# Second MoE layer in two stages with g in DRAM, and its output by seven products for eight

## The chip, the cores and the metric

The kernel runs on one core of a Trainium2 chip. The metric is device time in microseconds of one launch; the median of several runs counts. Engines: PE (TensorE), DVE (VectorE), ACT (ScalarE), POOL (GpSimd) and SP (SyncE, which here issues nearly all DMAs, in order).

## The reference

The kernel computes attention through a small memory, then two MoE-like layers, all in fp32:

```python
xn = x / rms * rms_g
g = xn @ w_gate;  silu = g * (1.0 / (1.0 + np.exp(-g)));  val = xn @ w_val
x = (silu * val) @ w_out                 # first layer, d_ff 1536
h = x @ w_in                             # second layer, d_ff 2048
out = np.maximum(h, 0.0) ** 2 @ w_out2
```

There are 4608 tokens of 512 values. The change touches the second layer and the work that prepares it.

## The kernel before, in words

Every fp32 operand of a matmul is split into a high and a low part (`split`: the high part on ACT, the low part on DVE or, where said, on POOL), and a product is three matmuls: high x high, high x low, low x high.

**First layer** (`phase_a`): 192 items n, 24 for each of 8 batches. An item is 12 matmuls of 288 columns for g and v, one silu on ACT, a product on DVE, a split (low part on POOL) and 12 matmuls into y for the item before. At four places of an item, `slot` runs steps of a plan. In the last batch (n = 168 to 191) the loop also loads x for the second layer and makes its sums (`x2_step`, one an item), and the first W_in set.

**Second layer** (`phase_b`): tokens go in four pairs of blocks of 512 and a last pair of 256. For each pair, eight steps q each take two slices of 128 hidden values of W_in. A 2x2 block product (two token blocks by two slices, split also along the 512 values) is done by seven products for eight: A11·X11, A12·X21, S2·T2, S3·T3, S1·T1, S4·X22, A22·T4, with S sums of W_in blocks and T sums of x blocks. A product is six matmuls (two kk of 128 values), so a step is 42. DVE combines the results into four blocks of h, relu and square give g.

The output g·W_out is plain: `mm_z` (L1184 to L1186), three matmuls of 128x512 for each slice f and each 128 tokens. For the first block of a pair (`z`) g stays in SBUF, and pieces of four `mm_z` stand between the h products; for the second block (`zz`) g goes to DRAM (`gd`), comes back on ACT's queue (`gb`), is split and multiplied after the pair's steps. W_in is loaded and split again for every pair (its S sums come back split from DRAM, `sd`). The 16 slices of W_out are split at the start of this stage (`wo2_next`). The order on each engine is the order in which the code is written (manual_schedule). A DMA on SP also waits for the eighth DMA before it.

## Time and profile before

| | us |
|---|---|
| median of three runs | 1612.98 (1611.53 to 1613.99) |
| span of the profiled execution | 1610.1 |
| first matmul of the second layer | at 853.30 |
| last matmul | at 1603.54 |

The profiled execution's own time is its span; the runs' median lies 2.9 us above it. The profile counts an engine as busy while instructions of it run; matmuls overlap in their pipeline, so that the distance between two starts, not the printed duration, says what one more matmul costs. PEclk is the TensorE clock that was granted, in tenths of full speed; windows give it as a fraction.

### The profile page before, as it was taken

What the parts mean: (1) busy time and instruction counts of PE and PEld (TensorE: products, weight loads), DVE (VectorE), ACT (ScalarE), POOL (GpSimd) and SP (SyncE); (2) the same over time, 40 slices, a digit from 0 to 9 for tenths busy, and PEclk for the clock granted to TensorE, in tenths of its full rate; (3) what the DMA queues carried; (4) which work ended last, traced back from release to release, by engine and by line L of the source; (5) the groups of instructions that cost most, each with busy time, mean ns of one, the idle gap of its engine ahead of it and who ended that gap; (6) DMA issues with size and microseconds to landing.
All of it is one profiled execution on the core that took longest, in us unless ns stands there. A gap on an engine that the chain in (4) does not pass through costs nothing.

```text
span 1610.1 us, 26490 instructions
## 1 busy us (share of the span) xinstructions
PE 1556.0 (97%) x10298; PEld 1311.0 (81%) x10298; DVE 953.7 (59%) x1645; ACT 592.8 (37%) x1208; POOL 386.6 (24%) x415
## 2 busy tenths in 40 slices
PE   6788999999999999999999999999999999999998
PEld 3556798888979889898998887888788878887887
DVE  5755645657365465625457876666666655666465
ACT  2666435354453544434343334211321133122322
POOL 0475534344353444333322210000000000000000
PEclk7688999999999999999999999999999999999999
DMA  9997583654657464324124465345534453445353
GB/s 265 281 310 279 196 233 134 211 189 154 189 205 200 166 187 140 118 71 146 55 75 172 174 240 168 96 140 179 176 116 144 155 179 108 158 160 177 97 165 99
DMA packets 143021, 269.92 MB, mean 168 GB/s; under 512 B 30704, under 2 KB 72944, under 8 KB 136752
## 3 DMA queue, kind: packets, MB, share of 16 engines
q1 hardware_dynamic: 129440, 248.43, 47.4%
q10 hardware_dynamic: 13328, 19.54, 4.1%
q8 instruction: 81, 1.33, 0.3%
q14 instruction: 44, 0.36, 0.1%
q0 software_dynamic: 128, 0.26, 0.1%
HBM read 208.28 MB, written 59.90 MB: 167 GB/s over the span
## 4 chain that ended last, share of the span: by engine, by line
PE 84%; DVE 5%; DMA 3%; ACT 3%; POOL 1%; issue 1%; SPq 0%; ACTq 0%; POOLq 0%; DVEq 0%
PE y L827 6%; PE y L828 5%; PE y L829 5%; PE z L1184 5%; PE z L1186 5%; PE z L1185 4%; PE h_S L1020 4%; PE h_S L1018 4%; PE h_S L1019 4%; PE zz L1186 3%; PE v L811 3%; PE h_A L1018 3%; PE zz L1185 3%; PE zz L1184 3%; PE h_A L1020 3%; PE h_A L1019 3%
## 5 line engine op out<-in xcount | busy, mean ns | idle before, releaser
L71 POOL TENSOR_TENSOR ul<-sl,uh 128x288 fp32r<-128x288 f32 x192 | 163.1, 850 | 387.2 <-ACT uh L67 384.2
L827 PE MATMUL y<-uh,woh 128*128 128x288 f32 x768 | 236.8, 308 | 0.0
L828 PE MATMUL y<-uh,wol 128*128 128x288 f32 x768 | 228.7, 298 | 0.0
L829 PE MATMUL y<-ul,woh 128*128 128x288 f32 x768 | 227.4, 296 | 0.0
L861 DVE TENSOR_TENSOR sl<-sl,v 128x288 f32<-128x288 f32 x192 | 86.2, 449 | 209.2 <-PE v L813 153.2
L67 ACT ACTIVATE gh<-c 128x512 fp32r<-128x512 f32 (+1 forms) x96 | 53.8, 561 | 404.2 <-DVE c L1053 395.9
L827 PEld LDWEIGHTS y<-uh,woh 128*128 128x128 f32 x768 | 146.0, 190 | 17.7 <-issue 16.8
L1192 POOL DMA_DIRECT2D out_dram<-os_last x4 | 2.2, 552 | 656.5 <-DVE os_last L1203 656.5
L828 PEld LDWEIGHTS y<-uh,wol 128*128 128x128 f32 x768 | 146.5, 191 | 0.7
L829 PEld LDWEIGHTS y<-ul,woh 128*128 128x128 f32 x768 | 146.0, 190 | 0.0
L67 ACT ACTIVATE uh<-sl 128x288 fp32r<-128x288 f32 x192 | 85.2, 444 | 163.6 <-DVE sl L861 162.9
L857 ACT ACTIVATE sl<-g 128x288 f32<-128x288 f32 x192 | 78.5, 409 | 170.7 <-PE g L813 163.0
L811 PE MATMUL g<-anh,wph 128*128 128x288 f32 x384 | 119.2, 310 | 12.3 <-ACT sl L857 9.9
L1184 PE MATMUL z<-bzh,gh 128*128 128x512 f32 x320 | 126.1, 394 | 0.0
L1186 PE MATMUL z<-bzh,gl 128*128 128x512 f32 x320 | 125.7, 393 | 0.0
L1185 PE MATMUL z<-bzl,gh 128*128 128x512 f32 x320 | 125.0, 391 | 0.0
L811 PE MATMUL v<-anh,wph 128*128 128x288 f32 x384 | 120.0, 312 | 1.7 <-DVE sl L861 1.7
L812 PE MATMUL v<-anl,wph 128*128 128x288 f32 x384 | 115.0, 299 | 0.0
L812 PE MATMUL g<-anl,wph 128*128 128x288 f32 x384 | 114.9, 299 | 0.1
L813 PE MATMUL v<-anh,wpl 128*128 128x288 f32 x384 | 114.7, 299 | 0.0
L813 PE MATMUL g<-anh,wpl 128*128 128x288 f32 x384 | 113.7, 296 | 0.0
L556 DVE TENSOR_TENSOR wpl<-wp,wph 128x512 fp32r<-128x512 f32 x96 | 61.4, 682 | 87.0 <-ACT wph L550 86.9
(217 smaller groups left out, 3749.5 us busy)
## 6 DMA issues: line engine op xcount, KB each, us to landing
w<-w SPq DMA_DIRECT2D x48, 1024.0 KB, 6.7
si<-w_i SPq DMA_DIRECT2D x80, 256.0 KB, 2.8
q<-in_q_dram SPq DMA_DIRECT2D x128, 144.0 KB, 5.1
gd<-c SPq DMA_DIRECT2D x64, 256.0 KB, 2.0
gb<-gd ACTq DMA_DIRECT2D x64, 256.0 KB, 3.6
y<-ys SPq DMA_DIRECT2D x16, 576.0 KB, 3.3
raw_i<-in_moe_w_in_dram SPq DMA_DIRECT2D x16, 512.0 KB, 4.1
raw_z<-in_moe_w_out_dram SPq DMA_DIRECT2D x16, 512.0 KB, 4.4
```

The costliest lines, as they stand in the source:

```text
L67: nc.scalar.activation(hi, src, AF.Copy)
L71: eng.tensor_tensor(lo, src, hi.bitcast(F32), op=ALU.subtract)
L811: nc.tensor.matmul(out, wh[:, r, cs], ah[:, r], start=(r == 0), stop=False)
L812: nc.tensor.matmul(out, wh[:, r, cs], al[:, r], start=False, stop=False)
L813: nc.tensor.matmul(out, wl[:, r, cs], ah[:, r], start=False, stop=(r == NR - 1))
L827: nc.tensor.matmul(y, hi[:, cs], uh, start=first, stop=False)
L828: nc.tensor.matmul(y, lo[:, cs], uh, start=False, stop=False)
L829: nc.tensor.matmul(y, hi[:, cs], ul, start=False, stop=last)
L1018: nc.tensor.matmul(out, wh[:, cs], xh, start=(kk == 0), stop=False)
L1184: nc.tensor.matmul(y[c], gh[:, cs], oh, start=(f == 0), stop=False)
L1185: nc.tensor.matmul(y[c], gh[:, cs], ol, start=False, stop=False)
L1186: nc.tensor.matmul(y[c], gl[:, cs], oh, start=False, stop=(f == NF2 - 1))
```

## The change

- **Preparation in the last batch.** From item 171 on, `slot` runs one piece of a list at each of its four places. The list (`last_batch`) has the two times seven x steps, all eight sets of W_out and two of W_in. A set is two raw slices (256 KB each, two buffers shared with x, `xr`), four sums of 128x256 on POOL that go where nothing else is kept, three splits (a, c, b of 256 or 512, and 1024 columns), and a store of the split set, 128x3584 or 1.8 MB, to DRAM (`wd`), followed on SP by the load of the set after next.
- **h stage** (`phase_h`). The steps of pairs 0 and 1 run interleaved, then those of 2, 3 and 4, by the strings in `STEPS`, so a W_in set serves two or three pairs. Sets 2 to 7 are made in the first group and read back from DRAM in the second. All of g goes to DRAM. Relu and square are two ACT passes for three of four blocks. Products rotate over eight PSUM banks. For pairs 1 to 4 the differences of x are on POOL.
- **Output stage** (`phase_z`). 18 runs of 128 rows (of both blocks of a pair), each in four groups of two q. A group loads g (two DMAs of 128x4x128), makes four sums (two DVE, two POOL), splits 1792 columns (ACT, DVE) and does seven products of 128x256 for two q, three matmuls each: 42. `z_out` combines them after a run. W_out sets T0 to T7 are loaded in the last steps of the h stage (`wt_load`) into the buffers of pairs 2 and 3's x sums; the g load of every third group uses that of pair 4's.

PE, where before an output piece follows a step's second product:

```order
L1018 MATMUL h_1_A_10531<-X21h_1_10068,wiha_10452 128x512
L1019 MATMUL h_1_A_10531<-X21l_1_10069,wiha_10452 128x512
L1020 MATMUL h_1_A_10531<-X21h_1_10068,wila_10453 128x512
L1184 MATMUL z_0_10518<-bzh_10396,gh_0_10439 128x512
L1185 MATMUL z_0_10518<-bzl_10397,gh_0_10439 128x512
L1186 MATMUL z_0_10518<-bzh_10396,gl_0_10440 128x512
L1184 MATMUL z_1_10519<-bzh_10396,gh_0_10439 128x512
L1185 MATMUL z_1_10519<-bzl_10397,gh_0_10439 128x512
L1186 MATMUL z_1_10519<-bzh_10396,gl_0_10440 128x512
L1018 MATMUL h_1_S_10551<-T2h_0_9864,wihb_10468 128x512
```

PE at the end of the last h step, where the output stage now begins (Wr is W_in read back, T an output-weight set, S the split sums of g):

```order
L1081 MATMUL h_7_A_13819<-x_41_11424,Wr_13214 128x256
L1082 MATMUL h_7_A_13819<-x_41_11424,Wr_13214 128x256
L1083 MATMUL h_7_A_13819<-x_41_11424,Wr_13214 128x256
L1275 MATMUL z_0_13839<-T_13364,S_13610 128x256
L1276 MATMUL z_0_13839<-T_13364,S_13610 128x256
L1277 MATMUL z_0_13839<-T_13364,S_13610 128x256
L1275 MATMUL z_0_13839<-T_13364,S_13610 128x256
L1276 MATMUL z_0_13839<-T_13364,S_13610 128x256
L1277 MATMUL z_0_13839<-T_13364,S_13610 128x256
L1275 MATMUL z_1_13840<-T_13364,S_13610 128x256
L1276 MATMUL z_1_13840<-T_13364,S_13610 128x256
L1277 MATMUL z_1_13840<-T_13364,S_13610 128x256
```

The output matmuls have left the h steps, and are of 256 columns.

ACT in the last batch before (sl is the silu, uh and X.. or T.. high parts):

```order
L67 ACTIVATE X22h_1_10105<-xr_1_9945 128x512
L857 ACTIVATE sl_10116<-g_10109 128x288
L67 ACTIVATE uh_10126<-sl_10116 128x288
L67 ACTIVATE T3h_1_10144<-xt_1_10142 128x512
L857 ACTIVATE sl_10155<-g_10148 128x288
L67 ACTIVATE uh_10165<-sl_10155 128x288
L67 ACTIVATE T1h_1_10182<-xr_1_9945 128x512
L857 ACTIVATE sl_10193<-g_10186 128x288
L67 ACTIVATE uh_10203<-sl_10193 128x288
```

ACT there now, with the last two W_in sets (Wi, made from si):

```order
L79 ACTIVATE uh_10243<-sl_10231 128x288
L79 ACTIVATE Wi_10240<-si_10159 128x256
L79 ACTIVATE Wi_10240<-si_10159 128x1024
L898 ACTIVATE sl_10281<-g_10263 128x288
L79 ACTIVATE uh_10293<-sl_10281 128x288
L79 ACTIVATE Wi_10297<-si_10219 128x512
L79 ACTIVATE Wi_10297<-si_10219 128x256
L79 ACTIVATE Wi_10297<-si_10219 128x1024
L898 ACTIVATE sl_10322<-g_10313 128x288
L79 ACTIVATE uh_10337<-sl_10322 128x288
L898 ACTIVATE sl_10360<-g_10353 128x288
L79 ACTIVATE uh_10370<-sl_10360 128x288
```

The high parts of three pieces of a weight set stand between the silus of successive items.

SP in the last batch before:

```order
L843 DMA y_13_84<-ys_9433 128x1152
L980 DMA xr_0_9594<-y_0_71 128x2x288
L980 DMA xr_0_9594<-y_1_72 128x2x224
L980 DMA xr_0_9594<-y_1_72 128x2x64
L980 DMA xr_0_9594<-y_2_73 128x2x288
L980 DMA xr_0_9594<-y_3_74 128x2x160
L922 DMA si_0_9600<-w_i_93 128x512
L922 DMA si_1_9602<-w_i_95 128x512
L843 DMA y_14_85<-ys_9913 128x1152
L980 DMA xr_1_9945<-y_0_71 128x2x288
```

SP there now (wdz are the stored sets, sz the raw slices):

```order
L100 DMA wdz_9519<-Wz_9833 128x3584
L956 DMA sz_9871<-w_z_106 128x512
L956 DMA sz_9871<-w_z_108 128x512
L100 DMA wdz_9520<-Wz_9893 128x3584
L956 DMA sz_9924<-w_z_110 128x512
L956 DMA sz_9924<-w_z_112 128x512
L100 DMA wdz_9521<-Wz_9948 128x3584
L956 DMA sz_9984<-w_z_114 128x512
L956 DMA sz_9984<-w_z_116 128x512
L884 DMA y_14_85<-ys_10038 128x1152
L100 DMA wdz_9522<-Wz_10005 128x3584
```

Each store stands ahead of the load of the set after next.

SP at the end of the h stage now:

```order
L1171 DMA gd_6_9564<-c_4_6_13733 128x256
L1171 DMA gd_6_9564<-c_4_6_13710 128x256
L1013 DMA T_13757<-wdz_9524 128x3584
L1171 DMA gd_7_9565<-c_4_7_13766 128x256
L1013 DMA T_13771<-wdz_9525 128x3584
L1171 DMA gd_7_9565<-c_4_7_13802 128x256
L1171 DMA gd_7_9565<-c_4_7_13814 128x256
L1171 DMA gd_7_9565<-c_4_7_13791 128x256
L1216 DMA sr_13829<-gd_4_9530 128x4x128
L1216 DMA sr_13829<-gd_5_9531 128x4x128
L1216 DMA sr_13832<-gd_6_9532 128x4x128
L1216 DMA sr_13832<-gd_7_9533 128x4x128
```

The loads of the last two output-weight sets and the last g stores stand ahead of the g loads of group 2 (sr).

The diff, cut:

```diff
+NQ = NF2 // 2
+NPAIR = NB // 2 + 1
+PART = 7 * 2 * P
...
+STEPS = [
+    [(p, int(q)) for name, q in zip(names[::2], names[1::2]) for p in [order.index(name) + base]]
+    for order, base, names in (
+        ("AB", 0, "A0A1A2B0B1A3B2A4B3A5B4A6A7B5B6B7"),
+        ("ABC", 2, "A0A1A2B0C0B1C1A3B2C2A4B3C3A5B4C4A6A7B5C5B6B7C6C7"),
+    )
+]
...
-        eng.tensor_tensor(lo, src, hi.bitcast(F32), op=ALU.subtract)
+        self.after(partial(eng.tensor_tensor, lo, src, hi.bitcast(F32), op=ALU.subtract))
+
...
+        if self.later is None:
+            f()
+        else:
+            self.later.append(f)
...
+        low, self.low = self.low, []
+        self.later = self.low
+        if self.side:
+            self.side.pop(0)()
+        self.later = None
+        for f in low:
+            f()
...
+        self.wd = {(k, q): dram.tile([P, 2 * PART], F32, name=f"wd{k}{q}") for k in "iz" for q in range(NQ)}
+        self.gd = [
+            [dram.tile([P, 4, self.width(p)], F32, name=f"gd{p}_{q}") for q in range(NQ)] for p in range(NPAIR)
+        ]
+        self.w2_raw, self.w2_out, self.wi, self.wt, self.x2, self.xr = {}, {}, {}, {}, {}, {}
+        self.side = self.last_batch()
...
-            self.phase_b()
+            self.phase_h()
+            self.phase_z()
...
+        if n >= NI * (B - 1) + 3:
+            self.piece()
...
-                self.x2_load(0, 0)
...
-            elif i == 13:
-                self.x2_load(0, 1)
-            if 6 <= i < 13:
-                self.x2_step(0, 0, i - 6)
-            elif 15 <= i < 22:
-                self.x2_step(0, 1, i - 15)
-            elif i == 5:
-                self.wi2_sums(0, 0)
-            elif i in (13, 14, 22):
-                self.wi2_split(0, 0, "abc"[(13, 14, 22).index(i)])
-            elif i == 23:
-                self.wi2_load(0, 1)
-                self.wo2_next(0)
...
+        out = [partial(self.chain, partial(self.x2_load, 0, 0), load("z", 0))]
+        out += then(x2(0), partial(self.x2_load, 0, 1)) + then(self.w2_pieces("z", 0, 0), load("z", 1))
+        out += then(x2(1), load("z", 2))
+        for q in range(1, NQ):
+            after = load("z", q + 2) if q < NQ - 2 else load("i", q + 2 - NQ)
+            out += then(self.w2_pieces("z", q, q % 2), after)
+        out += then(self.w2_pieces("i", 0, 0), partial(self.x2_load, 1, 0))
+        out += then(self.w2_pieces("i", 1, 1), load("i", 2))
+        return out
...
+        t = self.wb.tile([P, 2, 2, DM], F32, tag="xr", bufs=2, name=f"s{kind}{q}")
         for i in range(2):
...
+            self.nc.sync.dma_start(t[:, 0, i], self.w2d[kind, 2 * q + i])
...
+        out = [partial(self.w2_sums, kind, q, i) for i in range(2)]
+        return out + [partial(self.w2_split, kind, q, slot, part) for part in "acb"]
...
+            eng.tensor_tensor(s[:, 3], a12, s[:, 1], op=ALU.subtract)
+        elif half == 0:
+            eng.tensor_tensor(s[:, 0], a12, a11, op=ALU.subtract)
+            eng.tensor_tensor(s[:, 1], a22, s[:, 0], op=ALU.subtract)
+        else:
+            eng.tensor_tensor(s[:, 2], a22, a12, op=ALU.subtract)
+            eng.tensor_tensor(s[:, 3], s[:, 1], a21, op=ALU.subtract)
...
+        if part == "a":
+            self.w2_out[kind, q] = self.w_tile(slot, f"W{kind}{q}")
...
-            for x, d in zip(t, self.sd[q]):
-                self.nc.sync.dma_start(d, x.bitcast(F32))
+            src, o = raw[:, 1].rearrange("p a n -> p (a n)"), 3 * n
+        elif kind == "i":
+            src, o = (s0, 0) if part == "a" else (s1[:, n:DM], 2 * n)
+        else:
+            src, o = (s0[:, 0:n], 0) if part == "a" else (s1, n)
+        e = o + src.shape[-1]
+        self.split(t[:, o:e], t[:, PART + o : PART + e], src)
+        if part == "b":
+            del self.w2_raw[kind, q]
+            if kind == "i":
+                self.wi[q] = t
+            self.after(partial(self.nc.sync.dma_start, self.wd[kind, q], t.bitcast(F32)))
...
+        t = self.w_tile((NQ + q) % 3, f"Wr{q}")
+        self.nc.sync.dma_start(t.bitcast(F32), self.wd["i", q])
...
+        pool = self.wb2 if q // 4 else self.wb
+        t = pool.tile([P, 2 * PART], F32R, tag=f"x{q // 4}_{q % 4}", name=f"T{q}")
+        self.nc.sync.dma_start(t.bitcast(F32), self.wd["z", q])
...
+        eng = nc.gpsimd if p else nc.vector
...
+        self.split(hi, lo, x, lo_engine="pool" if p and i in (2, 3) else "dve")
...
+        at(0, "A0", x2(1, 0), xl(1, 1))
+        at(0, "A1", w2(2), wl(3))
+        at(0, "A2", x2(1, 1), wl(4))
+        at(0, "B1", w2(3), wl(5))
...
+        at(1, "A1", x2(3, 0, 5), partial(self.s_load, 0))
+        at(1, "A1", x2(3, 1, 0, 3))
+        at(1, "A2", x2(3, 1, 3), partial(self.s_load, 1))
...
+            plan[g, k].insert(0, partial(self.wi_load, q))
+        for q, name in enumerate(("B5", "C5", "B6", "B7", "C6", "C6", "C7", "C7")):
+            at(1, name, [partial(self.wt_load, q)])
+        at(1, "B6", self.s_sums(0))
+        at(1, "B7", self.s_split(0))
+        at(1, "C6", self.s_sums(1))
+        at(1, "C7", self.s_split(1))
...
+        tags = ("g", "v", "att", "att", "y0", "y1", "y2", "y3")
...
+            def store(c, blk, engine="act"):
+                if engine == "act":
+                    nc.scalar.activation(c, c, AF.Relu)
+                    nc.scalar.activation(c, c, AF.Square)
...
-                c11 = work("c", 4, f"c11_{p}_{q}", w)
-                nc.vector.tensor_tensor(c11, b2, p1, op=ALU.add)
...
-                    self.wi2_split(np, nq, "a")
-                piece()
-                b5 = product("S1", "T1")
-                nc.vector.tensor_tensor(u, b5, u, op=ALU.add)
...
-                self.mm_z(y, self.gs[p, f0], f0, c)
-            if not wide:
...
-            for f in range(NF2 + 1):
-                gb_load(f + 7)
-                if f < NF2:
-                    self.gs.pop((p, f), None)
-                    key = ("b", p, f)
-                    hi = self.wb2.tile([P, T], F32R, tag="uh", bufs=3, name=f"gbh{p}_{f}")
-                    lo = self.wb2.tile([P, T], F32R, tag="ul", bufs=3, name=f"gbl{p}_{f}")
-                    self.split(hi, lo, loaded[f])
-                    self.gs[key] = (hi, lo)
-                if f:
-                    self.pieces += z_pieces(2 * p + 1, y, ("b", p, f - 1), f - 1)
...
+                    nc.vector.scalar_tensor_tensor(c, c, 0.0, c, op0=ALU.max, op1=ALU.mult)
+                nc.sync.dma_start(self.gd[p][q][:, blk], c)
+
+            b1 = product("A11", "X11")
+            p1 = work("cp", 3, f"p1_{p}_{q}")
+            nc.scalar.activation(p1, b1, AF.Copy)
...
+            c11 = work("c", 6, f"c11_{p}_{q}")
+            nc.vector.tensor_tensor(c11, b2, p1, op=ALU.add)
+            store(c11, 1)
...
+            t = self.wb.tile([P, 8, 2, P], F32, tag="xr", bufs=2, name=f"sr{g}")
+        else:
+            t = self.wb2.tile([P, 8, 2, P], F32, tag="x4_1", name=f"sr{g}")
+        for i in range(2):
+            self.nc.sync.dma_start(t[:, 0:4, i, :], self.gd[p][2 * qg + i][:, :, r * P : (r + 1) * P])
...
+            if first:
+                nc.vector.tensor_tensor(t[:, 6], t[:, 1], t[:, 0], op=ALU.subtract)
+                nc.vector.tensor_tensor(t[:, 5], t[:, 3], t[:, 6], op=ALU.subtract)
+                nc.gpsimd.tensor_tensor(t[:, 4], t[:, 0], t[:, 3], op=ALU.add)
+            else:
+                nc.gpsimd.tensor_tensor(t[:, 7], t[:, 2], t[:, 5], op=ALU.subtract)
...
+            t = self.sr.pop(g)[:, 1:8].rearrange("p i q n -> p (i q n)")
+            o = self.w_tile((g + 1) % 3, f"S{g}")
+            self.split(o[:, 0:PART], o[:, PART : 2 * PART], t)
...
+        for f in [partial(self.s_load, 2), partial(self.s_load, 3)] + self.s_sums(2):
+            f()
...
+            self.s_load(g + 4)
+            side = self.s_sums(g + 3) + self.s_split(g + 2)
+            s = self.ss.pop(g)
...
+                    nc.tensor.matmul(out, sh, th, start=first, stop=False, **kw)
+                    nc.tensor.matmul(out, sh, tl, start=False, stop=False, **kw)
+                    nc.tensor.matmul(out, sl, th, start=False, stop=last, **kw)
+
+                mm(0, 0, 0, 0)
+                mm(0, 1, 6, 2)
...
+        o0 = self.wb2.tile([P, T], F32, tag="c", bufs=6, name=f"o{run}_0")
+        nc.vector.tensor_tensor(pair(o0), pair(z1), twice(p1), op=ALU.add)
+        u = self.wb2.tile([P, T], F32, tag="cp", bufs=3, name=f"zu{run}")
+        nc.vector.tensor_tensor(pair(u), pair(z2), twice(o0[:, n:T]), op=ALU.add)
...
+        nc.vector.tensor_tensor(o0[:, n:T], z0[:, n:T], u[:, n:T], op=ALU.add)
+        self.out_rows(p, r, 0, o0, (nc.sync, nc.gpsimd) if last else (nc.sync,))
+        nc.vector.tensor_tensor(o1[:, n:T], z2[:, n:T], u[:, 0:n], op=ALU.add)
+        nc.vector.tensor_tensor(o1[:, 0:n], u[:, 0:n], z3[:, 0:n], op=ALU.subtract)
+        self.out_rows(p, r, 1, o1, (nc.scalar, nc.sync) if last else (nc.sync,))
```

## Rows read from the trace of the kernel before

**Rows 1.** The page: busy time by engine, and the granted clock in 40 slices.

```profile
PE 1556.0 (97%) x10298; PEld 1311.0 (81%) x10298; DVE 953.7 (59%) x1645; ACT 592.8 (37%) x1208; POOL 386.6 (24%) x415
...
PEclk7688999999999999999999999999999999999999
```

**Rows 2.** Windows: busy time of each engine, granted clock, DMA share, GB/s.

```profile
core 0: us, PE busy (x) PEld busy (x) DVE busy (x) ACT busy (x) POOL busy (x), PEclk, DMA share, GB/s
772.00:808.00 36.00, 36.00 (x279) 34.98 (x279) 12.12 (x21) 14.48 (x33) 13.34 (x18) 1.00 0.19 61
...
853.30:1603.80 750.50, 747.81 (x3410) 615.16 (x3408) 486.40 (x808) 199.21 (x375) 22.54 (x25) 1.00 0.46 153
```

**Rows 3.** Timeline of PE: first matmuls of two steps with no piece between.

```profile
1014.86 0.39 PE L1018 MATMUL h_A<-X11h,wiha 128*128 128x512 f32 x1
...
1030.03 0.40 PE L1018 MATMUL h_A<-X11h,wiha 128*128 128x512 f32 x1
```

**Rows 4.** Groups by form: output matmuls of first and second blocks, busy, mean ns.

```profile
L1184 PE MATMUL z<-bzh,gh 128*128 128x512 f32 x320 | 126.1, 394 | 0.0
...
L1184 PE MATMUL zz<-bzh,gbh 128*128 128x512 f32 x256 | 100.3, 392 | 2.1 <-ACT gbh L67 2.1
```

**Rows 5.** Timeline of PE: matmuls of 288 and of 256 columns in a row.

```profile
702.74 0.30 PE L811 MATMUL g<-anh,wph 128*128 128x288 f32 x1
...
703.94 0.29 PE L811 MATMUL v<-anh,wph 128*128 128x288 f32 x1
...
1527.55 0.28 PE L1018 MATMUL h_S<-T2h,wihb 128*128 128x256 f32 x1
...
1528.97 0.39 PE L1184 MATMUL z<-bzh,gh 128*128 128x512 f32 x1
```

**Rows 6.** Timeline of DVE and ACT in the last batch; 835.18 is item 187.

```profile
787.32 0.46 DVE L861 TENSOR_TENSOR sl<-sl,v 128x288 f32<-128x288 f32 x1 [2.73 <-PE v L813]
790.54 0.45 DVE L861 TENSOR_TENSOR sl<-sl,v 128x288 f32<-128x288 f32 x1 [2.76 <-PE v L813]
...
835.18 0.41 ACT L857 ACTIVATE sl<-g 128x288 f32<-128x288 f32 x1 [0.66 <-PE g L813]
```

**Rows 7.** Timeline of POOL: the four sums of a W_in set, twice.

```profile
850.56 0.74 POOL L938 TENSOR_TENSOR si_s<-si 128x256 f32<-128x256 f32 x1
...
852.76 0.74 POOL L941 TENSOR_TENSOR si_s<-si,si_s 128x256 f32<-128x256 f32 x1
...
872.27 0.74 POOL L938 TENSOR_TENSOR si_s<-si 128x256 f32<-128x256 f32 x1 [18.77 <-DMA si<-w_i]
...
875.32 0.74 POOL L941 TENSOR_TENSOR si_s<-si,si_s 128x256 f32<-128x256 f32 x1
```

**Rows 8.** Groups by form: splits of W_in and a difference of x, busy, mean ns.

```profile
L67 ACT ACTIVATE wiha<-si 128x512 fp32r<-128x512 f32 x40 | 24.7, 617 | 0.0
...
L71 DVE TENSOR_TENSOR wilc<-si,wihc 128x256 fp32r<-128x256 f32 x40 | 17.1, 428 | 0.8 <-ACT wihc L67 0.8
...
L71 DVE TENSOR_TENSOR wilb<-si_s,wihb 128x1024 fp32r<-128x1024 f32 x8 | 9.8, 1221 | 1.8 <-ACT wihb L67 1.8
L67 ACT ACTIVATE wihb<-si_s 128x1024 fp32r<-128x1024 f32 x8 | 8.5, 1057 | 9.3 <-POOL si_s L941 9.2
...
L997 DVE TENSOR_TENSOR xt<-xr 128x512 f32<-128x512 f32 x8 | 5.5, 686 | 0.0
```

**Rows 9.** DMA issues (KB each, us to landing), and windows as in rows 2.

```profile
si<-w_i SPq DMA_DIRECT2D x80, 256.0 KB, 2.8
...
xr<-y SPq DMA_DIRECT2D x14, 288.0 KB, 4.1
...
sd0h<-wihb SPq DMA_DIRECT2D x1, 512.0 KB, 3.4
...
60.00:80.00 20.00, 14.17 (x213) 10.60 (x213) 16.23 (x26) 13.36 (x25) 10.65 (x9) 0.63 0.83 258
100.00:120.00 20.00, 15.82 (x110) 12.56 (x102) 12.21 (x20) 11.60 (x24) 15.13 (x13) 0.91 1.05 323
824.00:826.00 2.00, 2.00 (x17) 2.00 (x16) 0.97 (x2) 1.36 (x3) 0.81 (x1) 1.00 1.05 409
```

More of the change, by code (lines that the diff above doesn't have):

```diff
@@ new lines, in last_batch, with x2, then, load @@
+    def last_batch(self):
+        def x2(kk):
+            return [partial(self.x2_step, 0, kk, i) for i in range(7)]
+        def then(pieces, *loads):
+            return pieces[:-1] + [partial(self.chain, pieces[-1], *loads)]
+        def load(kind, q):
+            return partial(self.w2_load, kind, q)
+        out = [partial(self.chain, partial(self.x2_load, 0, 0), load("z", 0))]
[7 more added lines that the diff above has]
+        return out
@@ L1004, in x2_step @@
         else:
             k, x = "T4", x21
[L1006 to L1012 removed]
+            eng.tensor_tensor(x, x21, x22, op=ALU.subtract)
+        j = X_ORDER.index(k)
+        hi, lo = (self.x2[p, kk, hl][:, j, 0:w] for hl in range(2))
```

451 lines of the change are left out of this document (209 added, 242 removed).

## The prediction

> **What bounds the kernel now.** I read the page's busy shares first: PE is busy 97% of the span, and its granted clock is at nine tenths or more in all slices but the first four [rows 1]. Then the windows: from the first product of the second layer, 853.30, to its last, PE works 747.81 of 750.50 us, with DVE at 486 and ACT at 199 [rows 2]. So this stage is a chain of matmuls with no holes; it gets shorter only by fewer columns, and any work of DVE, ACT, POOL or DMA that fits beside PE is free. The batch before it is the same: 36.00 of 36.00 us busy [rows 2], one item each 3.22 us [rows 6]. There too the change can only add. Its order is therefore: what do fewer columns give, and does the preparation that pays for them fit?
>
> **Part 1, columns.** Before, the second layer has 1344 h matmuls of 512 columns (4 pairs x 8 steps x 42), 336 of 256 (last pair), and (320 + 256) x 3 = 1728 output matmuls of 512 [rows 4]. The prices: an h step without pieces runs from 1014.86 to 1030.03 with 66 matmuls of 512, so 15.17 / 66 = 0.2298 us [rows 3]; twelve matmuls of 256 take 1528.97 − 1527.55 = 1.42, 0.1183 each [rows 5]. The durations that the rows print (0.39, 0.28) overlap; the distance of starts is the price. h costs 1344 x 0.2298 + 336 x 0.1183 = 348.6 and stays. The output part now is 750.5 − 348.6 = 401.9. After, it is 72 groups (18 runs of 128 rows from both blocks of a pair, four groups of q each; 7 products x 2 q x 3 matmuls = 42 in a group), 3024 matmuls of 256: 3024 x 0.1183 = 357.7. **Gain 44.2.** Bounds: nine matmuls of 288 take 1.20 [rows 5], 0.1333 each; scaled from 288 to 256 with the slope between 256 and 288 unknown, 0.1194 at worst (gain 41); a price strictly by columns, 0.2298 / 2 = 0.1149, would gain 54, but the twelve of 256 already show more, so I end the range half way, at 49.
>
> **Part 2, the last batch.** The W_in of two steps, all eight output-weight sets and their sums are now made there, one piece per slot, four slots an item. 85 slots hold 65 pieces, so by slots it fits. By engine time it does too: ten sets need POOL 10 x 2.94 (four sums, 850.56 to 852.76 + 0.74 [rows 7]). What does not fit is the chain through two raw buffers. A set's raw is 0.52 MB, its sums overwrite half of the buffer, and SP, which issues in order, has: store of set q (1.835 MB, waits for the last low part), load of set q+2, store of q+1. So each buffer goes round like this:
> - landed to last low part: sums 2.94, hi of 128x1024 1.06, lo 1.22 [rows 7, 8], hand-overs 0.3: 5.5;
> - low part to landed: store and load, 2.36 MB at 409 GB/s, the most that a window shows while transfers queue [rows 9], 5.77; a 256 KB load takes 2.8 on its own [rows 9], of which 0.64 is this rate's transfer, so 2.1 fixed; issue 0.3: 8.2.
>
> A round is 13.7 us and makes two sets; their ten pieces stand in 2.5 items, 8.0 us of PE. The preparation falls behind PE by 5.7 us a round.
>
> The start: seven x2 pieces, now four an item, need seven low parts and four differences of 0.69 [rows 8] on DVE, 7.6 us against 5.6 by slots. By hand: first x2 set done 793.1, second load landed 798 and done 806.6, last low part of set z1 809.6, so z3 landed 817.8, and with three more rounds (z5, z7, i1) i1 landed 858.9. PE feels it through ACT: the wide hi part of i1 stands on ACT ahead of the silu of item 187, and the low parts of POOL behind the sums. Sums and hi, 4.3, put that silu at 863.2; now it starts at 835.18 [rows 6]. That is 28.0, of which 2.4 is PE's lead over ACT: **+26**. Bounds: +13.5 if the lag of DVE and the hand-overs vanish and only the transfers count; +34 if sums take the 3.79 that they take from 872.27 to 875.32 + 0.74, beside DVE [rows 7], on each round, with the lag.
>
> A rule bears on this. The Trainium skill (GPSIMD Engine Reference, section 1, Specifications) says that POOL shares its SBUF interfaces with VectorE and contends with DVE instructions that read two SBUF inputs, which every low part does. Rows 7 agree in kind: 2.94 alone, 3.79 beside DVE. By the rule on every set the stage would give the +34.
>
> **Part 3, the start of the output stage.** Let E be the end of the last h step. The output-weight sets T4 to T7 go into the buffers of pair 3's X sums, free only when pair 3 ends, two steps of 42 x 0.1183 = 4.97 before E. They are 7.34 MB, 17.9 us at 409 GB/s; with 2.1 fixed and the g stores between them on SP, 1.2, T7 lands at E + 11.3. The load for group 2 uses a buffer of pair 4's X sums, free at E, and stands behind T7 on SP: landed about E + 15.7 (issue 0.3 and the 4.1 that a strided load of 288 KB takes [rows 9]). Its two DVE sums (0.43 each [rows 8]), the last POOL sum 0.74, hi of 1792 columns (1.057 + 768 x 0.44/512 = 1.72) and lo (2.02 the same way) end at E + 21. Groups 0 and 1 keep PE until E + 9.9. **+11**, bounds +4 (the load overtakes T7 on the 16 queues) and +15 (rate of rows 9's slower window).
>
> **Part 4, the rest.** The h stage loses its mix of pieces: a step is 42 x 0.2298 = 9.65 us of PE, in which ACT at the fullest has 14 passes of 0.617 (one copy, three relu and three square, seven hi), 8.6; DVE seven combinations, one relu-square and five low parts, 9.0; POOL four differences and two low parts, 5. That is under 9.65 with eight banks rotating: **0**, bounds −4 and +6. Its DMA, 1.05 MB of g and at most 1.8 MB of weights a step, is 7 us at 409 GB/s: covered by the same step; without that cover a reload would hold PE directly. In the output stage a group is 4.97 of PE against ACT 1.7 plus a share of the combination, DVE 3.5, POOL 1.5 to 2.5, DMA 1.3: covered. What ran beside PE before (z's splits, W_in prepared for each pair, gb loads, the 128 stored rows) costs and gives nothing. After a stall the clock has to rise again: rows 9 show 0.63 while PE is busy 14.17 of 20 us, so two stalls of 10 to 26 us may be followed by slow stretches, **+2** (0 to 6).
>
> **Sum.** 1610.1 − 44.2 + 26 + 11 + 2 = 1604.9 for the profiled execution. The median of the runs, 1612.98, lies 2.9 above that execution: **1608**.
>
> **The rivals.**
> A (slower): the transfers do not get 409 GB/s. That row is 2 us long; in the long full window 100 to 120 the 16 DMA engines are at 1.05 of their time at 323 GB/s [rows 9]. Against it: those early transfers are in smaller pieces. At 323 store and load take 7.3 instead of 5.77, over 3.5 rounds +5.4, and part 3 another +4.8: 1618. It decides against me from about 335 GB/s down, where the sum crosses 1616.
> The Trainium skill (DMA: Bandwidth & Descriptors, Specifications) gives about 358 GB/s as the HBM limit for one core; the row with 409 lies over that, in a window too short to be sure. By 358 the sum would be 1613.
> B (slower): TensorE falls to its 1.2 GHz level inside the last batch, as PE then works 8.0 us in 13.7, 58%; rows 9 show 0.63 at 71%. At half the clock the work of a round takes 16 us rather than 8.0, more than the 13.7, so PE, not the chain, sets the pace: four rounds of 16 − 13.7 give +9, and up to +13 with the climb behind them; at +12, 1620. Against it: PE's work comes in bursts at full density, unlike the first stage's.
> C (faster): both stalls are mostly hidden, by transfers of several queues overlapping (last batch +13.5, start of output +5, clock 0): 1610.1 − 44.2 + 18.5 + 2.9 = 1587. For it: sd0h's 512 KB land in 3.4 [rows 9], nearly without a fixed part if they overlap.
> D (slower): the h steps with x2 pieces become DVE's or ACT's, eleven steps by 1 us: 1619. Against: 9.0 of 9.65.
> That seven products don't replace eight is excluded by the order below the change: 42 matmuls of 256 a group.
>
> **Chances.** Forecast (1600 to 1616) 0.38, A 0.20, B 0.17, C 0.20, D 0.05. A measurement of this kernel can tell about 0.2%, 3.2 us: faster is under 1609.8, slower over 1616.2. Faster: C 0.20 and 0.22 of the forecast, which has 1608 just below the bound; same: 0.16 of it and 0.06 of A; slower: the rest of A, B, D, 0.36. Range: from C's 1587 to 1630 (B with the upper bound of part 3), leaving 2 in 10 out.
>
> **What would show it.** Right: 3024 output matmuls with starts 0.118 apart; PE idle 20 to 30 us between 800 and 865 in several holes, released by ACT's silu or POOL's low parts behind raw loads; one hole of about 11 us some 10 us after the last h matmul, released by the split of group 2; h steps of 9.65 us. Wrong: store plus load well under or over 8.2 us from issue to landing, PEclk near 0.5 in the last batch (B), holes inside h steps (D), or a cadence over 0.12.

## The result, and the profile after

The changed kernel takes 1627.47 us (median of four runs, 1626.42 to 1628.44); the kernel before, on the same chip, 1612.8. The ratio is 1.0089, with a 95% interval of 1.0075 to 1.0104: slower by 0.9%, where 0.3% faster was forecast. The time lies inside the whole range (1587 to 1630), but over the 1600 to 1616 of the forecast itself, and on the wrong side of the kernel before.

The page of the changed kernel shows PE less busy in all than before (1530.5 us against 1556.0 [rows 1]) in a longer span, and the clock, behind the first four slices, below nine tenths in two places (slice 21, and slices 31 and 32):

```profile
PE 1530.5 (94%) x11594; PEld 1353.6 (83%) x11594; DVE 1016.8 (63%) x1548; ACT 733.0 (45%) x1304; POOL 639.6 (39%) x637
...
PEclk7788999999999999999989999999998899999999
```

The windows part the second layer into the last batch, the h stage, the start of the output stage and its rest (columns as in rows 2):

```profile
820.00:870.00 50.00, 36.70 (x218) 34.52 (x217) 24.34 (x32) 20.72 (x41) 31.92 (x37) 0.86 0.95 345
...
885.94:1242.20 356.26, 349.92 (x1682) 291.03 (x1680) 246.19 (x379) 194.42 (x353) 82.75 (x75) 1.00 0.67 229
1242.20:1275.00 32.80, 18.71 (x108) 17.77 (x107) 12.12 (x15) 7.18 (x9) 8.31 (x7) 0.72 0.78 294
1275.00:1620.27 345.27, 345.27 (x2920) 345.23 (x2919) 264.76 (x288) 122.30 (x86) 149.36 (x134) 1.00 0.45 127
```

The last row is the gain as it was meant: 2920 matmuls in 345.27 us, 0.1182 each, no hole. The first row is the last batch: PE works 36.70 of 50 us at a granted clock of 0.86, where it worked 36.00 of 36.00 at 1.00 before [rows 2], and the DMA engines are 0.95 busy. The third row is the start of the output stage: 18.71 of 32.80 us at 0.72.

The timeline of PE has the borders and the holes (the bracket is the idle time before, and what ended it):

```profile
885.94 0.39 PE L1081 MATMUL h_A<-x,Wi 128*128 128x512 f32 x1
...
923.08 0.50 PE L1082 MATMUL h_S<-x,Wi 128*128 128x512 f32 x1 [2.12 <-DVE x L100]
...
1188.66 0.47 PE L1081 MATMUL h_A<-x,Wr 128*128 128x512 f32 x1 [1.19 <-DMA Wr<-wdi]
...
1247.51 0.58 PE L1275 MATMUL z<-T,S 128*128 128x256 f32 x1 [5.14 <-DVE c L1193]
...
1252.10 0.58 PE L1275 MATMUL z<-T,S 128*128 128x256 f32 x1 [1.66 <-DVE c L1198]
...
1268.59 0.58 PE L1275 MATMUL z<-T,S 128*128 128x256 f32 x1 [5.96 <-ACT S L79]
...
1270.70 0.58 PE L1277 MATMUL z<-T,S 128*128 128x256 f32 x1 [1.32 <-DVE S L88]
...
1620.15 0.28 PE L1277 MATMUL z<-T,S 128*128 128x256 f32 x1
```

The first x load of the last batch is a mark that both kernels have on SP, so that what lies ahead of it (a us or two more or less from run to run) drops out; in both kernels 556 matmuls lie between it and the first h matmul. Before, then after:

```profile
778.51 3.48 SPq L980 DMA_DIRECT2D xr<-y  x5
```

```profile
780.17 3.46 SPq L1029 DMA_DIRECT2D xr<-y  x5
```

From there to the first h matmul (below: from mark to mark) it is 74.79 us before (853.30 − 778.51) and 105.77 after (885.94 − 780.17). So the budget of the 16.6 us between the spans is:

| stage | forecast | measured | from |
|---|---|---|---|
| fewer columns | −44.2 | −44.2 | 3024 matmuls at 0.1183 for 401.9 us; the last window above gives 0.1182 |
| ahead of the last batch | 0 | +1.7 | 780.17 − 778.51 |
| last batch | +26 | +31.0 | 105.77 − 74.79 |
| h stage | 0 | +7.7 | 356.3 (885.94 to 1242.2) − 348.6 |
| start of the output | +11, clock +2 | +20.4 | 378.1 (1242.2 to 1620.27) − 357.7 |

### The profile page after: what moved, and what is told of

Its sections match the earlier page's. It is cut to its first block, busy times and chain, and to the rows that moved or that the text cites. A ratio compares the mean times of both kernels' runs of the same rounds, so it can differ in the third digit from the quotient of the medians.

```text
span 1626.7 us, 29659 instructions
## 1 busy us (share of the span) xinstructions
PE 1530.5 (94%) x11594; PEld 1353.6 (83%) x11594; DVE 1016.8 (63%) x1548; ACT 733.0 (45%) x1304; POOL 639.6 (39%) x637
## 4 chain that ended last, share of the span: by engine, by line
PE 72%; DVE 8%; DMA 6%; ACT 5%; POOL 4%; issue 4%; SPq 0%; DVEq 0%; POOLq 0%; ACTq 0%
PE z L1277 7%; PE z L1275 7%; PE z L1276 7%; PE y L868 5%; PE y L869 5%; PE y L870 5%; PE v L852 3%; PE h_S L1082 3%; PE h_S L1083 3%; PE h_S L1081 3%; PE wp L571 3%; PE g L852 3%; PE v L853 2%; PE v L854 2%; PE g L853 2%
## 5 line engine op out<-in xcount | busy, mean ns | idle before, releaser
L88 POOL TENSOR_TENSOR ul<-sl,uh 128x288 fp32r<-128x288 f32 x192 | 168.7, 879 | 365.8 <-ACT uh L79 361.4
L1275 PE MATMUL z<-T,S 128*128 128x256 f32 x1008 | 286.8, 285 | 12.8 <-ACT S L79 6.0
L1277 PE MATMUL z<-T,S 128*128 128x256 f32 x1008 | 286.1, 284 | 1.3 <-DVE S L88 1.3
L1276 PE MATMUL z<-T,S 128*128 128x256 f32 x1008 | 286.0, 284 | 0.0
L79 ACT ACTIVATE S<-sr 128x1792 fp32r<-128x1792 f32 x72 | 122.6, 1703 | 205.4 <-PE z L1277 141.4
L1275 PEld LDWEIGHTS z<-T,S 128*128 128x128 f32 x1008 | 195.2, 194 | 13.5 <-ACT S L79 6.2
L1277 PEld LDWEIGHTS z<-T,S 128*128 128x128 f32 x1008 | 194.1, 193 | 1.6 <-DVE S L88 1.6
L1276 PEld LDWEIGHTS z<-T,S 128*128 128x128 f32 x1008 | 194.2, 193 | 0.0
L88 DVE TENSOR_TENSOR S<-sr,S 128x1792 fp32r<-128x1792 f32 x70 | 144.0, 2057 | 55.8 <-ACT S L79 55.8
L1231 POOL TENSOR_TENSOR sr<-sr 128x256 f32<-128x256 f32 x72 | 84.1, 1168 | 232.3 <-DVE sr L1228 232.3
L1167 ACT ACTIVATE c<-c 128x512 f32<-128x512 f32 (+1 forms) x120 | 70.1, 584 | 150.0 <-DVE c L1193 96.3
L1229 POOL TENSOR_TENSOR sr<-sr 128x256 f32<-128x256 f32 x72 | 77.6, 1078 | 133.0 <-DMA sr<-gd 123.9
```

The costliest lines, as they stand in the source:

```text
L79: nc.scalar.activation(hi, src, AF.Copy)
L88: f()
L1231: nc.gpsimd.tensor_tensor(t[:, 7], t[:, 2], t[:, 5], op=ALU.subtract)
L1275: nc.tensor.matmul(out, sh, th, start=first, stop=False, **kw)
L1276: nc.tensor.matmul(out, sh, tl, start=False, stop=False, **kw)
L1277: nc.tensor.matmul(out, sl, th, start=False, stop=last, **kw)
```

## The experiments

Each was run beside the kernel before. Most are single executions; their spans are compared with the 1626.7 of the changed kernel. The spans of one kernel scatter (four of the changed kernel from 1624.6 to 1626.7, ten of z_unsplit below from 1607.0 to 1613.8), so a few us in a single span show nothing, and the argument goes by stages. The edits are cut to the lines that carry them. A round is the time in which the last batch makes two weight sets.

**The stores of the last batch, taken away (no_store).**

```diff
-            self.after(partial(self.nc.sync.dma_start, self.wd[kind, q], t.bitcast(F32)))
+            if kind == "i":
+                self.after(partial(self.nc.sync.dma_start, self.wd[kind, q], t.bitcast(F32)))
 (wt_load)
-        self.nc.sync.dma_start(t.bitcast(F32), self.wd["z", q])
+        self.nc.sync.dma_start(t.bitcast(F32), self.wd["i", q])
```

> The eight output-weight sets are loaded, summed and split in the last batch as before, but not stored; T0 to T7 are read from the stored W_in sets, so the output is made with wrong weights and the work after the last batch is the same. Theory 1, transfers pace the last batch: a round of two sets (store to store, 14.0 us in the changed kernel) loses the 3.67 MB of two stores, which share the queues: 1.835 MB a chain link, 4.5 to 4.9 us, so rounds of 9.1 to 9.5; the first h matmul moves from 885.9 to about 869. Theory 2, the engines pace it (POOL sums beside DVE, ACT's and POOL's work in order behind them): rounds stay over 12.5 and the first h matmul comes later than 880.

Span 1616.5. From the first x load to the first h matmul 97.31: 8.5 less, half of what theory 1 said. The rounds (from one low part of 1024 columns to the next but one, 815.65 to 851.49 in three) are 11.9. In the changed kernel the same three rounds take 13.7 each (814.98 to 856.09, from store to store), and four, with the W_in sets at their end, 14.0 (to 870.91). The window, and POOL's waits from 816 to 852 (us in total, times, longest), answer why:

```profile
820.00:870.00 50.00, 40.84 (x275) 37.95 (x274) 28.38 (x37) 23.45 (x48) 40.45 (x42) 0.97 0.47 158
```

```profile
POOL ul L88 <- ACT uh L79: 3.7, 4, 1.5
```

DMA is at 0.47, yet POOL works 40.45 of 50 us, with four sums a set and the low parts of the first layer in between, and it never waits for a load, only for ACT's high parts uh. Neither theory was right alone: behind the transfers stands POOL, 2 us a round shorter.

**The load ahead of the store (load_first).**

```diff
+                self.pend = store      # the store is queued after the loads of chain()
```

> Only the order on SP in the last batch changes: the load of set q+2 is issued ahead of the store of set q. Theory 1a, latency: the load waits for the store ahead of it; rounds fall from 14.0 to about 9.5 and the first h matmul from 885.9 to about 870. Theory 1b, bandwidth: the windows from 820 to 870 show the DMA engines 0.85 to 1.03 busy at 286 to 381 GB/s, and two sets are 4.72 MB; at 375 GB/s a round can't go below 12.6, so the first h matmul comes at 880 to 884. Theory 2, engines: no change within 2 us.

Span 1623.2; 104.23 from mark to mark, 1.5 less, rounds of 13.5 in three and 13.1 in four. The load landed earlier, but then ACT's high part waited for the store of the set that had used its output buffer (21.1 us from 800 to 872, none in the changed kernel), and the window shows 366 GB/s at a DMA share of 0.96. That speaks for theory 1b: the order alone hardly matters while the DMA engines are full. By size it can't be told from theory 2, as 1.5 us is within its 2, and the first h matmul, at 882.22 and so in theory 1b's range, owes 2.2 us to an earlier start.

**The sums, taken away (no_sums).**

```diff
-        out = [partial(self.w2_sums, kind, q, i) for i in range(2)]
+        out = [partial(self.w2_sums, kind, q, i) if kind == "i" else (lambda: None) for i in range(2)]
```

> The changed kernel without the POOL sums of the eight output sets in the last batch: the wide split reads the raw slices in their place, so loads, splits and stores are as many and as large, and the output is made with wrong weights. Theory 1, one serial chain (landing, sums, split, store and load): a round of 14.0 loses the 2.9 to 4 us of sums, 10 to 11, and the first h matmul comes 12 us earlier, near 874. Theory 2, two limits side by side, transfers (4.72 MB a round at 360 GB/s, 13.1) and POOL (no_store: 12): the round falls to 12.8 to 13.3 only, first h matmul 880 to 883. Theory 3, POOL's queue alone: rounds near 8, first h matmul before 868.

Rounds of 12.7 (815.70 to 853.70 in three, against 13.7), 101.80 from mark to mark, 4.0 less; the span, 1626.4, is no shorter than the changed kernel's, as this execution came to the last batch 2.4 us later and other stages vary by a us. The window:

```profile
820.00:870.00 50.00, 36.64 (x219) 34.51 (x218) 21.64 (x32) 20.76 (x42) 14.94 (x18) 0.86 0.96 359
```

POOL is down to 14.94 and DMA stays at 0.96, 359 GB/s. The round is theory 2's, and so is the first h matmul, at 884.40, once those 2.4 us are taken off. There are two limits side by side, transfers at about 12.7 and POOL at about 12, and a chain through both, 13.7 to 14.0. Taking one away leaves the other.

**The sums on DVE (dve_sums).**

```diff
-        eng = self.nc.gpsimd
+        eng = self.nc.vector if kind == "z" or q < 2 else self.nc.gpsimd
```

> The sums of the ten sets in the last batch are made on DVE (0.43 us each) instead of POOL; stores and loads are the same. Theory 1, transfers pace the last batch: sums shrink from 2.9 to 4 us to 1.7 in the chain, but 4.72 MB a round at 360 GB/s don't: rounds of 13 to 13.5, first h matmul 880 to 884. Theory 2, POOL paces it (no_store left rounds of about 12 with POOL 40 of 50 us busy): rounds of 11.5 or less, first h matmul before 878.

Both theories missed: span 1643.1, 126.33 from mark to mark, 20.6 more, rounds of 19.8. DVE's waits from 820 to 900 (us in total, times, longest) say it:

```profile
DVE sz L977 <- DMA sz<-w_z: 24.1, 5, 5.7
```

A sum that waits for its load holds DVE, and behind it on DVE stands the silu product of the same item, which ACT, POOL and then PE wait for. PE waits 26.3 us in this stretch for that product. On POOL the same waits (14.7 us from 800 to 872) had held up the first layer's low parts, for which PE waited nowhere in that stretch of the changed kernel.

**The end of the h stage in another order (t_order).**

```diff
-        ("ABC", 2, "...A6A7B5C5B6B7C6C7"),
+        ("ABC", 2, "...A6A7B5B6B7C5C6C7"),
-        for q, name in enumerate(("B5", "C5", "B6", "B7", "C6", "C6", "C7", "C7")):
+        for q, name in enumerate(("B5", "B6", "B6", "B7", "C5", "C5", "C6", "C6")):
```

> The last steps of the h stage run as B5 B6 B7 C5 C6 C7 instead of B5 C5 B6 B7 C6 C7, so pair 3 ends one 256-wide step earlier and T4 to T7 are issued at C5 and C6. Theory 1, the start of the output stage is held by T4 to T7 on SP, behind which the g stores (and so the buffers that DVE's additions need) and the load of group 2 stand: the holes of 5.1, 1.7, 6.0 and 1.3 us fall to under 6 in all, and with the clock the span goes from 1626.7 to about 1614. Theory 2, the order on DVE (low part of S1 ahead of the last additions): the first hole stays at 3 us or more. Theory 3, bandwidth alone: holes of 8 to 10, 1621.

The split of S0 moved along, from step B7 to C6, so this is two changes in one. Span 1622.2, holes in the output stage 9.4 instead of 14.1, but 2.0 of a new one just before its start: theory 3's size. The first hole stays too, at 5.7, as theory 2 said; so this run doesn't part the two. DVE still waits for g stores (6.3 us in three waits, 1225 to 1256).

**The output weights on another queue (t_pool).**

```diff
-        self.nc.sync.dma_start(t.bitcast(F32), self.wd["z", q])
+        self.nc.gpsimd.dma_start(t.bitcast(F32), self.wd["z", q])
```

> T0 to T7 are issued on POOL's DMA queue instead of SP's; order of work otherwise unchanged. Theory 1, the queue: the g stores no longer stand behind the T loads, so the holes of 5.1 and 1.7 us at the first output matmuls go and the load of group 2 is issued near the end of the last h step instead of 11.7 us after it; 1616 to 1620. Theory 2, bandwidth (7.3 MB in the last ten microseconds): the hole ahead of group 2 stays at 6 or more and the first ones shrink by less than half; 1624 to 1627.

Span 1627.1: nothing gained. The first hole doubled, and the issues of 1195 to 1262 (KB each, us to landing) show that the g stores, now free to be issued, land no sooner: 10.8 us, where those of the same size take 3.0 in the changed kernel.

```profile
1260.83 0.58 PE L1275 MATMUL z<-T,S 128*128 128x256 f32 x1 [10.46 <-DVE c L1193]
```

```profile
gd<-c SPq DMA_DIRECT2D x15, 256.0 KB, 10.8
```

Theory 1, the queue, falls. Theory 2 had the span, but not the holes: the first one grew, and the one ahead of group 2 fell to 1.4, as PE came to it later.

**Half of the output weights (t_half).**

```diff
-        self.nc.sync.dma_start(t.bitcast(F32), self.wd["z", q])
+        self.nc.sync.dma_start(t[:, 0:PART].bitcast(F32), self.wd["z", q][:, 0:PART])
```

> T0 to T7 are loaded by half: the high parts only (0.92 MB instead of 1.84), and the output matmuls read the high part where they should read the low one, so the output lacks the low parts of the weights; nothing else changes. Theory 1, bandwidth in the last 50 us of the h stage (14.7 MB of T and 4.7 MB of g at about 360 to 420 GB/s): with 7.3 MB less the g stores land in time and so does the load of group 2; holes at the start of the output stage from 14.1 us to under 4, the span from 1626.7 to 1608 to 1612. Theory 2, the order of ACT and DVE (splits of S0 and S1 ahead of the last additions): holes stay at 6 or more, 1618 to 1622.

Span 1611.1. From the last h matmul to the last output matmul 365.5 instead of 378.1, so 12.6 less (the other 3.0 lie ahead of the last batch: its first x load is at 777.15). Two holes are left, 5.5 us:

```profile
1243.67 0.58 PE L1275 MATMUL z<-T,S 128*128 128x256 f32 x1 [4.38 <-DVE c L1193]
...
1258.01 0.38 PE L1277 MATMUL z<-T,S 128*128 128x256 f32 x1 [1.15 <-DVE S L88]
```

So the bytes make the hole ahead of group 2 and the lower clock behind it, theory 1; the first hole stays without them, as theory 2 said: here DVE waited 1.7 us for the high part of S1 and split 2.0 us ahead of the last additions.

**The preparation moved out of the last batch (z_late).** The eight output sets are made in the second group of the h stage, one in each of eight wide steps:

```diff
-        out = [partial(self.chain, partial(self.x2_load, 0, 0), load("z", 0))]
+        out = [partial(self.chain, partial(self.x2_load, 0, 0), partial(self.x2_load, 0, 1))]
+        out += spread(then(x2(0), load("i", 0)) + then(x2(1), load("i", 1)), 2)
 (h_plan)
+        for q, name in enumerate(("B1", "A3", "B2", "A4", "B3", "A5", "B4", "A6")):
+            at(1, name, self.z_pieces(q), partial(self.w2_load, "z", q + 2) ...)
```

> The eight output-weight sets leave the last batch and are made in the second group of the h stage (one set in each of eight 512-wide steps, low parts in place, stored as before); the last batch keeps the x steps and two W_in sets, spread over its slots; steps end as in t_order. Theory 1, the last batch's 31 us are the price of those sets there: 4 us are left, the h stage takes them beside PE (its DMA was 0.3 to 0.75 busy there), 1622 less 27 is 1595. Theory 2, the h stage has no room (1.84 MB of stores and 0.5 MB of loads a step beside 1.05 MB of g and 1.8 MB of W_in): h holes of 10 or more, 1605 or slower.

Span 1666.1. From mark to mark 76.13, 1.3 over the kernel before: the sets are the price of the last batch, as theory 1 said. But the h stage took 431.2 instead of 356.3: theory 2's side, but not for bandwidth, as the DMA engines were 0.63 busy at 223 GB/s from 1060 to 1230. DVE's, ACT's and SP's waits from 1060 to 1230:

```profile
DVE sz L100 <- ACT zh L79: 72.5, 17, 7.4
```

```profile
ACT zh L79 <- DMA wdz<-zh: 74.6, 16, 6.8
```

```profile
SPq L1187 <- ACT c L1184: 65.9, 18, 6.8
```

The high parts had one small buffer, stored three times a set; each waits for a store, the low part on DVE waits for it, and the additions stand behind the low part.

**The sets stored unsplit (z_unsplit).** Half the bytes, and no split in those steps: high and low parts are made after the load (`wt_split`).

```diff
+            self.nc.sync.dma_start(d[:, 0:n], raw[:, 0:n])
+            self.nc.sync.dma_start(d[:, n:PART], raw[:, 2 * n : 8 * n])
 (wt_split)
+        self.split(t[:, 0:PART], lo, lo.bitcast(F32), lo_engine=lo_engine)
```

> As z_late, but the sets are stored unsplit (0.92 MB) and split after their load, high part on ACT, low part in place on DVE or POOL, in the last h steps and the first output group; steps end in the order of the changed kernel. Theory 1, bandwidth was what held the start of the output stage: holes there under 5 us and the last batch's extra time under 6: 1584 to 1590. Theory 2, the eight splits (1.7 us ACT, 2.05 DVE or over 5 POOL each) come too late for the first output groups or hold the last additions: holes of 8 to 15, 1595 to 1600.

1611.61 us, ratio to before 0.9999 (0.9987 to 1.0011): no difference, and slower than both theories. The h stage took 370.4. DVE's timeline and SP's waits (1085 to 1262) name a new wait:

```profile
1133.24 0.42 DVE L1216 TENSOR_TENSOR c<-h_S,u 128x256 f32<-128x256 f32 x1 [7.31 <-DMA gd<-c]
```

```profile
SPq L970 <- DMA wdz<-sz: 27.8, 6, 6.6
```

SP stood still for a raw load that waits for the store ahead of it, and g stores, whose buffers DVE needs, stood behind it.

**That load a step later (z_sp).**

```diff
-            at(1, name, self.z_pieces(q), partial(self.w2_load, "z", q + 2) ...)
+            if q:
+                at(1, name, [partial(self.w2_load, "z", q + 1) if q < NQ - 1 else partial(self.s_load, 0)])
+            at(1, name, self.z_pieces(q))
```

> As z_unsplit, but in the second group of the h stage the raw load of an output set is issued a step later, when its buffer has long been stored, instead of right behind the store that it waits for. Theory 1, SP in order: in z_unsplit that load held SP 27.8 us in all, the g stores stood behind it, DVE waited for their buffers and PE for DVE (holes of 2.2, 2.5 and 6.8 us); here the h stage falls from 370.4 to 357 to 359 us and the span from 1608.3 to about 1596. Theory 2, bandwidth or DVE's load in that stretch (DMA share 0.64 to 0.87): the h stage stays over 364.

Span 1595.5, h stage 356.7, where theory 1 had 357 to 359 and 1596. The holes at the start of the output stage, 13.1, are as in z_unsplit (13.0). The first two have one cause, DVE's last additions that wait for g stores, 1.7 and 6.9 us:

```profile
1222.46 0.42 DVE L1219 TENSOR_TENSOR c<-h_S,u 128x256 f32<-128x256 f32 x1 [6.88 <-DMA gd<-c]
```

**Two ways to mend that (z_tuned and z_two).** First the loads spread and the low parts moved to POOL:

```diff
+        for q, name in enumerate(("B6", "B6", "B7", "B7")):
+            at(1, name, [partial(self.wt_split, q, ("dve", "pool")[q % 2])])
+        at(1, "C7", [partial(self.wt_split, 4, "dve")])
```

> z_sp with steps that end B5 B6 B7 C5 C6 C7, T4 to T7 issued one at a time in C5 and C6, and the low parts of S0, S1, T1, T3, T5 and T7 on POOL. Theory 1, the last holes come from the four T loads that stand together ahead of the last g stores (7.1 us wait of DVE for a g store in z_unsplit): holes at the start of the output stage from 13.0 to under 5, span about 1585. Theory 2, DVE and POOL have no room for eight splits there (low part on POOL takes over 4 us, DVE was 0.88 to 0.99 busy from 1200 to 1220 and 1250 to 1260): holes of 8 or more in the last h steps or the first groups, 1592 to 1598.

1602.08 us, ratio 0.9941 (0.9925 to 0.9958), where the one run of z_sp took 1597.29: no better, and by theory 2's way. The split of T4 came ahead of the last additions. T4 had long landed (issued at 1203.56, 5.8 us to landing), but its high part stood on ACT behind that of S1, and this one waited for a sum that stood on POOL behind a low part of 4.0 us:

```profile
1220.01 1.70 ACT L79 ACTIVATE S<-sr 128x1792 fp32r<-128x1792 f32 x1 [4.48 <-POOL sr L1255]
```

```profile
1224.08 3.64 DVE L100 TENSOR_TENSOR T<-T 128x1792 fp32r<-128x1792 f32 x1 [7.76 <-ACT T L79]
```

PE lost 15.4 us at the first output matmul. Then, starting again from z_sp, two of the four loads put behind the last g stores:

```diff
-        for q, name in enumerate(("B5", "B5", "C5", "C5", "C6", "C6", "C6", "C6")):
+        for q, name in enumerate(("B5", "B5", "C5", "C5", "C6", "C6")):
+            partial(self.s_load, 2), partial(self.wt_load, 6), partial(self.s_load, 3), partial(self.wt_load, 7), ...
```

> z_sp with T6 and T7 issued after the last g stores and the load of group 2, the split of T4 after the last additions, the low parts of T4 to T7 on DVE in the order of their use. Theory 1, the last g stores stand behind T4 to T7 on the DMA engines (DVE waits 6.9 us for one in z_sp): holes at the start of the output stage from 13.1 to 6 or less, 1585 to 1588. Theory 2, what comes late is the work of DVE and ACT in the first two groups: the hole only moves to group 2 or 3, 1592 to 1597.

1593.42 us, ratio 0.9881 (0.9864 to 0.9897): 1.2% faster than the kernel before, 34 us under the changed kernel. The first holes are down to 3.3 us, theory 1, and others have grown at groups 2 and 3, theory 2, so that 10.5 are left:

```profile
1215.74 0.39 PE L1305 MATMUL z<-T,S 128*128 128x256 f32 x1 [2.65 <-DVE c L1214]
...
1239.38 0.39 PE L1305 MATMUL z<-T,S 128*128 128x256 f32 x1 [2.48 <-ACT S L79]
...
1242.80 0.58 PE L1307 MATMUL z<-T,S 128*128 128x256 f32 x1 [2.91 <-DVE S L88]
```

Of the 44.2 us of the columns 16.9 remain in this execution (1610.1 − 1593.2); the start of the output still takes 16.2, the h stage 7.3, the last batch 1.4 and what lies ahead of it 2.3.

## Why the prediction was wrong

The columns gave what was forecast, and the three terms that pay for them were too small: the last batch by 5.0 us, the start of the output stage by 7.4, and the h stage, put at nothing, by 7.7. The largest failures are steps of the sum and not only sizes: part 3 gave the loads of T4 to T7 a start and a clear way that they did not have, and part 4 took busy times under the step's length for cover.

**Part 1, columns: right.** 0.1182 us a matmul against 0.1183, gain 44.2.

**Part 2, the last batch: +26 forecast, +31.0 measured; mechanism half right.** The round, 13.7, came out at 13.7 to 14.0, and its two legs are in the trace: from a store's issue to the landing of the load behind it 7.4 to 9.2 us (8.2 forecast; the landing is where POOL's first sum has waited for it), and from there to the next store of that buffer 5.8 to 6.6 (5.5). What failed is that the legs stand by themselves. Removing 4.5 us of store should then have given 9.2, and it gave 11.9; removing the sums should have given 10 to 11, and it gave 12.7. The two buffers share the DMA engines and POOL: a round moves 4.72 MB, which at the measured 345 to 366 GB/s is 12.9 to 13.7 us by itself, and POOL holds a round at about 12. The rate was the mis-sized term: 409 GB/s was read from two microseconds [rows 9], and the loaded stretch of 50 us gives 345 to 366 with the engines 0.95 busy. That the round was right is in part luck: a rate too fast for a buffer that was thought to have the engines to itself. Of the 5.0 us that were missed, 3.7 come from the start: the last low part of z1 was put at 809.6 and ended at 815.0, 1.7 of it from ahead of the batch. The rounds, four times 0.3 longer, add 1.1. At the start the hand timetable had x's second set begin when its load landed; it stands behind z0's wide split on DVE (its first low part at 800.71), and POOL was held beside DVE's low parts, as these two rows of POOL show (the same took 0.81 us in this stretch before):

```profile
791.51 2.51 POOL L88 TENSOR_TENSOR ul<-sl,uh 128x288 fp32r<-128x288 f32 x1 [3.88 <-ACT uh L79]
...
805.95 2.51 POOL L88 TENSOR_TENSOR ul<-sl,uh 128x288 fp32r<-128x288 f32 x1 [3.88 <-ACT uh L79]
```

The sums took 3.4 us in the rounds (822.37 to 825.81, and the next two sets the same), between the 2.94 alone and the 3.79 beside DVE of rows 7; the +34 that goes with 3.79 on every set was not reached.

Rival A's condition, a rate near 335 or lower, was nearly met. The rule of the Trainium skill beside it (DMA: Bandwidth & Descriptors, Specifications, about 358 GB/s) lies among these 345 to 366; the window from 1250 to 1260, mostly loads, shows 422 and lies over it.

Rival B's clock did fall: between the holes of the last batch many matmuls of 288 start twice as far apart (0.24 instead of 0.1333), some 10 us in all, and the window has 0.86. It is not shown that this cost time of its own: from 800 to 872 nothing in the chain of loads, sums, splits and stores waits for PE (the only wait for PE on DVE, ACT or POOL is 1.2 us, of a silu product), so that the round paced PE and not PE the round. No run held the clock up there.

**Part 3, the start of the output: +11 and +2 forecast, +20.4 measured.** The place was right and so was the last wait, the split of group 2. Let E be 1242.20, the end of the last h matmul. The split's low part ended at E + 28.5, where E + 21 was forecast. The step that failed is the timetable of T4 to T7. It let T4 start when pair 3 ends, at E − 9.9; T4 was issued at E − 4.5, behind pair 3's last g stores on SP, the first of which had waited 6.7 us for ACT. T7 was issued only when T4, the eighth DMA before it, had landed, and it landed itself after 15.6 us, at E + 20.0 instead of E + 11.3 (the last row is of the issues from 1246 to 1248):

```profile
1237.75 0.38 SPq L1013 DMA_DIRECT2D T<-wdz  x1
...
1246.61 0.32 SPq L1013 DMA_DIRECT2D T<-wdz  x1
```

```profile
T<-wdz SPq DMA_DIRECT2D x1, 1792.0 KB, 15.6
```

The load of group 2 was issued at E + 11.7, about as forecast, but among these transfers it took 10.0 us instead of 4.1, and DVE began on it at E + 22.5. In the sum g's stores only cost T7 1.2 us. In fact they share the DMA engines with T4 to T7: those of 128 KB took 11.2 us to land (median of eight, 1235 to 1262), and DVE's last additions waited for their buffers, and the banks of the first output matmuls for DVE:

```profile
1243.87 2.02 DVE L100 TENSOR_TENSOR S<-sr,S 128x1792 fp32r<-128x1792 f32 x1 [1.67 <-ACT S L79]
...
1247.03 0.42 DVE L1193 TENSOR_TENSOR c<-h_S,u 128x256 f32<-128x256 f32 x1 [0.80 <-DMA gd<-c]
...
1251.62 0.42 DVE L1198 TENSOR_TENSOR c<-h_S,u 128x256 f32<-128x256 f32 x1 [4.17 <-DMA gd<-c]
...
1264.72 0.42 DVE L1227 TENSOR_TENSOR sr<-sr 128x256 f32<-128x256 f32 x1 [11.88 <-DMA sr<-gd]
...
1268.57 2.08 DVE L88 TENSOR_TENSOR S<-sr,S 128x1792 fp32r<-128x1792 f32 x1 [0.61 <-ACT S L79]
```

Of the two first holes, 6.8 us, the g stores explain the second and 0.8 of the first; the rest of the first is the split of S1, which stands on DVE ahead of the last additions, as t_half shows, where 4.4 us of it stay. But as long as group 2 can't start before its split, these holes only bring forward an idle time that would come there anyway: group 2 began at 1268.59, which is 16.4 us later than two groups without a hole would have put it (9.9). Of the 20.4 us, 16.4 are this late start, 1.3 the hole behind it, and the other 2.7 matmuls at the lower clock, where part 4 had set aside 2. In all the holes are 14.1 us and the lower clock costs 6.3, of which 3.6 lie ahead of group 2, under its wait.

**Part 4, the h stage: 0 forecast, +7.7 measured, over the upper bound of 6.** Busy times under the step's 9.65 us were taken as cover. Seven holes of 0.4 to 2.1 us, 6.3 in all, come from order instead (the other 1.4 us stay open): a high or low part of the next pair's x or of a W_in set that is late for its first use, twice a W_in reload. Rival D, in small. z_unsplit and z_sp show what waits on SP cost this stage: 27.8 us of them, for one kind of load, made it 14 us longer.

The misses, 5.0 + 7.7 + 7.4 and the 1.7 ahead of the last batch, make the 21.8 us between 1604.9 and 1626.7. They all have one sign. Most are places where something is queued behind a waiting instruction and the sum had counted only durations; the longer rounds and the lower clock are not.
